# The last output tile of a linear-attention block: one add moved to GpSimd, two adds and two stores joined

## The chip, the cores and the metric

The kernel runs on one core of a Trainium2 chip. The metric is the device time of one execution in microseconds (us), the median over several runs. A core has five engines that run their own instruction streams and wait for each other through semaphores: TensorE (PE, matmuls and weight loads), VectorE (DVE), ScalarE (ACT), GpSimd (POOL) and SyncE (SP). SP only issues DMAs here; ACT issues some too.

## The reference

The input x has 2048 tokens of 640 features. It is normalised, goes through a linear attention with 32 heads and through a two-layer network with a ReLU, and the two results are combined with a residual:

```
xn = layernorm(x)
q, k, v = split(xn @ wqkv)                  # 32 heads of 20
phi(t) = where(t > 0, t + 1, exp(t)) + 1e-6
o = phi(q) @ (phi(k)^T @ v) / (phi(q) . sum(phi(k)) + 1e-6)
s = o @ wo
g = silu(relu(xn @ w1) @ w2)                # 1728 hidden features
out = x + s * g
```

## The kernel before

The kernel is written instruction by instruction. A small scheduler class (`Sched`) takes every operation in program order, with the resources that it reads (`R`) and writes (`W`), and works out which semaphores the issuing engine has to wait for. Each engine executes its own operations in the order in which they were written. A wait blocks everything behind it on the same engine. The same holds for a DMA: the engine whose queue issues it (SP or ACT) first waits for the data. Every DMA has a semaphore of its own, and at the very end SP waits for all of them (`wait_all_dma`).

The tokens form 16 tiles of 128 rows. The last stage works through pairs of tiles. For each tile, `U_sub` and `U_halves` (matmuls at L846 and L864) compute the network's second layer into PSUM, `gate` (L874, ScalarE) writes `g` = silu of it to SBUF as bf16, and then the output is made. A matmul group `s_mm` (L895) computes s for the tile: five matmuls per column piece, with the folded weight `wf`, into one PSUM bank. `s_out` then does three things for a piece of columns: VectorE multiplies the PSUM result by g into `tmpo` (L885), VectorE adds the residual x (`xre`) into `outb` (L888), and SP stores `outb` to the output in HBM (L891).

Where these output parts stand among the matmuls of the second layer is a table written out by hand (`hooks`). Fifteen tiles are done by `s_tile`, with two matmul groups of 320 columns, one multiply, one add and one store of all 640 columns. The sixteenth is done last, by `s_last`, and cut into three pieces of 224, 208 and 208 columns, each with its own PSUM bank, multiply, add and store:

```
LC = [0, 224, 432, 640]
LB = [2, 3, 4]
```

For the last tile all matmuls of the second layer are over before `s_mm` begins, and its g is written by the last `gate`. `NOUT` is the slot of `tmpo` and `outb` that only the last tile uses. Other lines that the text names are: L414 and L416 (statistics of the layer norm on VectorE and GpSimd), L501 (GpSimd's running sum of phi(k)), L525 (VectorE's sum that makes phi(k)) and L551 (a VectorE operation whose input tensor is in PSUM).

Of the kernel before, what the change touches and what calls it, by code (L numbers as in the profile page):

```python
# [4 lines left out]
ALU = mybir.AluOpType  # L5
# [15 lines left out]
class Sched:  # L21
# [69 lines left out]

    def _hazards(self, R, W):
        agents = []
        for key in R:
            st = self.res.get(key)
            if st is not None and st.w is not None:
                agents.append(st.w)
        for key in W:
            st = self.res.get(key)
            if st is not None:  # L100
                if st.w is not None:
                    agents.append(st.w)
                agents.extend(st.r.values())
        return agents

    def _update_res(self, agent, R, W):
        Rset = set(R)
        for key in R:
            st = self.res.get(key)
            if st is None:  # L110
                st = self.res[key] = _Res()
            rk = agent if agent[0] == "D" else agent[0]
            st.r[rk] = agent
            st.nread += 1
        for key in W:
            st = self.res.get(key)
            if st is None:
                st = self.res[key] = _Res()
            else:
                assert (st.w is None or st.nread > 0 or key in Rset or key in self.allow_unread  # L120
                        or (agent[0] == "PE" and st.w[0] == "PE")), (
                    "unread overwrite of %r by %r (prev writer %r)" % (key, agent, st.w))
            st.w = agent
            st.r = {}
            st.nread = 0

    def op(self, E, fn, R=(), W=(), extra=()):
        return self.group(E, [fn], R, W, extra)
# [80 lines left out]
def bass_recurrent_scan__linear_attn_block__dense_activation_relu__prompt_kernel(  # L209
# [9 lines left out]
    Bb, S, D = A_x.shape  # L219
# [11 lines left out]
    HN = D // 2  # L231
# [6 lines left out]
    out2 = out[0]  # L238
# [10 lines left out]
    xre = xn  # L249

    NOUT = 4
# [4 lines left out]
    outb = reg3[:, VC * D:(VC + NB) * D].rearrange("p (a n) -> p a n", a=NB)  # L256
    tmpo = reg3[:, (VC + NB) * D:(VC + 2 * NB) * D].rearrange("p (a n) -> p a n", a=NB)
# [50 lines left out]
    ps = [psT[:, 512 * i:512 * (i + 1)] for i in range(8)]  # L308

    def ps2(b, n):  # L310
        return psT[:, 512 * b:512 * (b + 2)].rearrange("p (a n) -> p a n", a=2)[:, :, 0:n]
# [4 lines left out]
    sc = Sched(nc, NDS)  # L316
    nds = [0]

    def dma(E, fn, R=(), W=(), extra=()):
        i = nds[0]  # L320
        nds[0] += 1
        return sc.dma(E, fn, i, R=R, W=W, extra=extra)

    def tok(t):
        return slice(P * t, P * (t + 1))
# [25 lines left out]
    def wk_load(k0, k1):  # L351
# [23 lines left out]
          R=[("ident",)], W=[("ident",)])  # L375
# [344 lines left out]
    for j in range(J):  # L720
        for n, item in enumerate(plans[j]):
# [21 lines left out]
            if n in kat[j]:  # L743
                t = kat[j][n]
# [10 lines left out]
            if j == J - 1 and n == 0:  # L755
                for c in range(VC):
                    r0 = VR * c if c < VC - 1 else D - P
                    dma("SP", lambda eng, c=c, r0=r0: eng.dma_start(wo_sb[:, c, :], A_wo[r0:r0 + P, :]),
                        W=[("wo", c)], extra=[last_norm[0]])
# [12 lines left out]
    for a in range(2):  # L772
# [3 lines left out]
            W=[("w2", a)], extra=[lastW1])  # L776
    for u in range(2):
        dma("ACT", lambda eng, u=u: eng.dma_start(w2l[64 * u:64 * (u + 1), :], B_w2[NF * P:FF, :]),
            W=[("w2l", u)], extra=[lastW1])
# [100 lines left out]
    LC = [0, 224, 432, 640]  # L880
    LB = [2, 3, 4]

    def s_out(t, os_, i, lo, hi, src, keys, na):
        shp = "p (a n) -> p a n"
        sc.op("DVE", lambda eng: eng.tensor_tensor(  # L885
            out=tmpo[:, os_, lo:hi].rearrange(shp, a=na), in0=src, in1=g_sb[:, t, lo:hi].rearrange(shp, a=na),
            op=ALU.mult), R=keys + [("g", t)], W=[("tmpo", os_, i)])
        sc.op("DVE", lambda eng: eng.tensor_tensor(out=outb[:, os_, lo:hi], in0=tmpo[:, os_, lo:hi],  # L888
                                                   in1=xre[:, t, lo:hi], op=ALU.add),
              R=[("tmpo", os_, i), ("xre", t // 4)], W=[("outb", os_, i)])  # L890
        dma("SP", lambda eng: eng.dma_start(out2[tok(t), lo:hi], outb[:, os_, lo:hi]), R=[("outb", os_, i)])  # L891

    def s_mm(t, lo, hi, b):
        i = t // 4
        sc.group("PE", [(lambda eng, c=c: eng.matmul(  # L895
            ps[b][:, 0:hi - lo], lhsT=pqT[:, c, tok(t)], rhs=wf[:, c, lo:hi],
            start=(c == 0), stop=(c == C - 1))) for c in range(C)],
            R=[("pqT", i, c) for c in range(C)] + wkeys, W=[("ps", b)])

    def s_tile(t, b):  # L900
        os_ = so[0] % NOUT
        so[0] += 1
        for a in range(2):
            s_mm(t, HN * a, HN * (a + 1), b + a)
        s_out(t, os_, 0, 0, D, ps2(b, HN), [("ps", b), ("ps", b + 1)], 2)

    def s_last(t):
        for i in range(3):
            lo, hi = LC[i], LC[i + 1]
            s_mm(t, lo, hi, LB[i])  # L910
            s_out(t, NOUT, i, lo, hi, ps[LB[i]][:, 0:hi - lo].unsqueeze(1), [("ps", LB[i])], 1)

    lastG = None
    for k in range(C):
# [1 line left out]
    for jx in range(4):  # L916
        dma("SP", lambda eng, jx=jx: eng.dma_start(
            xre[:, 4 * jx:4 * jx + 4, :], x2[512 * jx:512 * (jx + 1), :].rearrange("(t p) n -> p t n", p=P)),
            W=[("xre", jx)], extra=[lastG])

    def s_of(p, u, b):
        return lambda: s_tile(pairs[p][u], b)
# [29 lines left out]
    for p in range(8):  # L952
# [7 lines left out]
        if p % 2 == 0:  # L960
            U_halves(p)
            gate(p, 0)
            gate(p, 1)
    s_last(pairs[7][1])

    sc.wait_all_dma("SP", list(range(nds[0])))
# [30 lines left out]
```

## Time and profile before

| | us |
|---|---|
| median of 5 runs | 221.24 |
| lowest and highest | 221.06, 221.47 |
| the profiled execution's own time | 221.23 |
| its span, from the first to the last instruction | 220.0 |
| TensorE busy | 214.8 (98%) |
| VectorE busy | 119.8 (54%) |
| ScalarE busy | 83.6 (38%) |
| GpSimd busy | 43.4 (20%) |

The granted TensorE clock was 0.998 over the span. In the rows of the profile a line is written as L885, an engine by its short name, and a queue that issues DMAs with a q behind it (SPq, ACTq). Operands are written output<-input with the names of the tensors: `reg` stands for the large SBUF regions, in which `tmpo`, `outb`, `g` and `xre` lie, and `psT` for PSUM. A group's row gives the shapes as partitions x elements, a count, then the busy time in us and the mean length of one in ns, and then the idle time in front. A row of the timeline gives the start in us, the length in us, and what ran.

### The profile page before, as it was taken

The page shows a single profiled execution, that of the slowest core. Times are in us where ns is not written, and L with a number is a line of the kernel's source. Part 1 is how long each engine was busy: PE and PEld are TensorE (multiplying, and loading weights), DVE is VectorE, ACT ScalarE, POOL GpSimd, SP SyncE. Part 2 cuts the span into 40 slices and gives each one's busy share as a digit, 9 for nine tenths or more (in the row PEclk, how much of TensorE's full clock was granted, in tenths as well). Part 3 has the DMA queues.
Part 4 walks back from the last instruction along what each step waited for, and adds up shares of the span by engine and source line. Part 5 has one row for each costly group of instructions (what it writes and reads, how often), then busy time and mean ns, then how long its engine had stood idle before and what let it go on. Part 6 is the DMA issues. An engine that isn't in the chain of part 4 may idle for free.

```text
span 220.0 us, 3506 instructions
## 1 busy us (share of the span) xinstructions
PE 214.8 (98%) x1436; PEld 132.9 (60%) x1436; DVE 119.8 (54%) x222; ACT 83.6 (38%) x139; POOL 43.4 (20%) x68
## 2 busy tenths in 40 slices
PE   6999999999999999999999999999999999999994
PEld 6555554555545555444467777677767776777673
DVE  3999947789639999783702116930424240413234
ACT  4497665566665676554420000551021102110211
POOL 2278501120041699950000000000000000000000
PEclk9999999999999999999999999999999999999999
DMA  6987493811001243000099979922110100001011
GB/s 215 365 236 160 96 317 37 208 30 30 3 1 35 54 105 107 0 0 3 5 207 308 370 234 376 368 77 63 50 40 30 63 30 30 33 30 61 3 60 60
DMA packets 28565, 24.72 MB, mean 112 GB/s; under 512 B 12293, under 2 KB 27909, under 8 KB 28549
## 3 DMA queue, kind: packets, MB, share of 16 engines
q1 hardware_dynamic: 24965, 19.83, 31.6%
q10 hardware_dynamic: 3584, 4.67, 6.3%
q8 instruction: 11, 0.18, 0.3%
q14 instruction: 5, 0.04, 0.1%
HBM read 15.81 MB, written 5.24 MB: 96 GB/s over the span
## 4 chain that ended last, share of the span: by engine, by line
PE 95%; DVE 2%; DMA 1%; ACT 0%; issue 0%; DVEq 0%
PE psT L846 26%; PE psT L565 26%; PE psT L786 10%; PE psT L543 10%; PE psT L490 10%; PE psT L895 9%; DMA reg<-in_A_x_dram 1%; PE psT L864 1%; PE psT L582 1%; PE psT L816 1%; PE psT L801 1%; PE psT L673 1%; DVE regX L475 0%; PE psT L465 0%; DVE reg L885 0%; DVE stats L410 0%
## 5 line engine op out<-in xcount | busy, mean ns | idle before, releaser
L846 PE MATMUL psT<-reg,hT 128*128 128x320 bf16 x416 | 60.5, 299 | 0.0
L846 PEld LDWEIGHTS psT<-reg,hT 128*128 128x128 bf16 x416 | 40.3, 98 | 16.4 <-issue 1.1
L565 PE MATMUL psT<-reg 128*128 128x512 bf16 x195 | 46.0, 379 | 0.0
L885 DVE TENSOR_TENSOR reg<-psT,reg 128x640 bf16<-128x640 f32 (+2 forms) x18 | 13.5, 750 | 48.3 <-PE psT L895 47.0
L569 ACT ACTIVATE hT<-psT 128x512 bf16<-128x512 f32 x52 | 30.8, 604 | 18.2 <-PE psT L565 18.2
L565 PEld LDWEIGHTS psT<-reg 128*128 128x128 bf16 x195 | 18.9, 98 | 21.8 <-issue 0.4
L874 ACT ACTIVATE reg<-psT 128x640 bf16<-128x640 f32 x12 | 8.2, 702 | 44.7 <-PE psT L846 25.3
L543 PE MATMUL psT<-reg 128*128 128x512 bf16 x100 | 24.8, 379 | 0.0
L895 PE MATMUL psT<-reg,pqT 128*128 128x320 bf16 (+2 forms) x165 | 24.4, 295 | 0.0
L501 POOL TENSOR_TENSOR zacc<-zacc,reg 128x640 f32<-128x640 f32 x16 | 23.8, 1488 | 2.3 <-DVE reg L525 1.3
L786 PE MATMUL psT<-reg 128*128 128x320 bf16 x160 | 21.9, 299 | 0.0
L895 PEld LDWEIGHTS psT<-reg,pqT 128*128 128x128 bf16 x165 | 16.1, 98 | 5.8
L786 PEld LDWEIGHTS psT<-reg 128*128 128x128 bf16 x160 | 15.7, 98 | 6.2
L507 ACT ACTIVATE regE<-psT 128x640 bf16<-128x640 f32 x24 | 15.6, 701 | 9.1 <-PE psT L490 7.6
L490 PE MATMUL psT<-reg 128*128 128x320 bf16 x120 | 18.3, 299 | 0.0
L551 DVE TENSOR_SCALAR regE<-psT 128x512 bf16<-128x512 f32 x20 | 13.6, 679 | 8.2 <-ACT regE L550 8.2
L553 DVE SCALAR_TENSOR_TENSOR pqT<-regE 128x512 bf16<-128x512 bf16 x20 | 17.4, 869 | 0.7
L543 PEld LDWEIGHTS psT<-reg 128*128 128x128 bf16 x100 | 9.8, 98 | 11.6
L410 DVE BATCH_NORM_STATS2 stats<-reg 128x6 f32<-128x320 bf16 x32 | 14.2, 476 | 2.8 <-DMA reg<-in_A_x_dram 2.8
L490 PEld LDWEIGHTS psT<-reg 128*128 128x128 bf16 x120 | 11.7, 98 | 6.5 <-DMA reg<-reg 0.2
L791 DVE CAST reg<-psT 128x640 bf16<-128x640 f32 x5 | 4.1, 825 | 20.9 <-PE psT L786 20.9
L550 ACT ACTIVATE regE<-psT 128x512 bf16<-128x512 f32 x20 | 11.9, 597 | 8.8 <-PE psT L543 8.8
(67 smaller groups left out, 162.1 us busy)
## 6 DMA issues: line engine op xcount, KB each, us to landing
scr<-regE SPq DMA_DIRECT2D x4, 640.0 KB, 11.1
reg<-in_A_x_dram SPq DMA_DIRECT2D x4, 640.0 KB, 9.3
out_dram<-reg SPq DMA_DIRECT2D x15, 160.0 KB, 1.8
reg<-in_A_x_dram SPq DMA_DIRECT2D x13, 160.0 KB, 4.0
regE<-scr SPq DMA_DIRECT2D x4, 512.0 KB, 5.6
reg<-in_B_w_dram ACTq DMA_DIRECT2D x1, 1120.0 KB, 12.1
reg<-in_B_w_dram ACTq DMA_DIRECT2D x1, 1040.0 KB, 6.3
reg<-in_A_wo_dram SPq DMA_DIRECT2D x6, 160.0 KB, 3.2
```

The lines of the kernel that those rows point to most:

```text
L410: sc.op("DVE", lambda eng: eng.bn_stats(stats[:, t, a, :], xv[:, HN * a:HN * (a + 1)]), R=[("xin", t % XR)], W=[("stats", t, a)])
L490: fns.append(lambda eng, a=a, k=k, lhs=lhs: eng.matmul(ps[b + a][:, 0:HN], lhsT=lhs[:, k, tok(t)], rhs=wqk[:, k, D + HN * a:D + HN * (a + 1)],
L501: sc.op("POOL", lambda eng: eng.tensor_tensor(out=zacc[:, :], in0=zacc[:, :], in1=pk[:, t, :], op=ALU.add), R=[("zacc",), ("pk", t)], W=[( ...
L507: sc.op("ACT", lambda eng: eng.activation(out=o_.rearrange("p (a n) -> p a n", a=2), in_=ps2(b, HN), func=func, scale=scale), R=[("ps", b) ...
L543: sc.group("PE", [(lambda eng, k=k: eng.matmul(ps[b], lhsT=wqk[:, k, P * f:P * (f + 1)], rhs=xnT[:, k, schunk(j)], start=(k == 0), stop=(k ...
L551: sc.op("DVE", lambda eng: eng.tensor_scalar(out=r_, in0=ps[b], scalar1=0.0, scalar2=1e-6, op0=ALU.max, op1=ALU.add), R=[("ps", b), ("er_e ...
L553: sc.op("DVE", lambda eng: eng.scalar_tensor_tensor(out=pqT[:, f, schunk(j)], in0=e_, scalar=1.0, in1=r_, op0=ALU.min, op1=ALU.add), R=[(" ...
L565: a = sc.group("PE", [(lambda eng, k=k: eng.matmul(ps[b], lhsT=w1_sb[:, k, P * f:P * (f + 1)], rhs=src[:, k, :], start=(k == 0), stop=(k = ...
L569: sc.op("ACT", lambda eng: eng.activation(out=hT[:, f, schunk(j)], in_=ps[b], func=ACTF.Relu), R=[("ps", b)], W=[("hT", j, f)])
L786: fns.append(lambda eng, t=t, a=a: eng.matmul(ps[b + a][:, 0:HN], lhsT=xn[:, t, P * k:P * (k + 1)], rhs=pk[:, t, HN * a:HN * (a + 1)], sta ...
L846: sc.group("PE", [(lambda eng, f=f: eng.matmul(ps[b][:, 0:HN], lhsT=hT[:, f, tok(t)], rhs=w2_sb[:, f, HN * n:HN * (n + 1)], start=(f == 0 ...
L895: sc.group("PE", [(lambda eng, c=c: eng.matmul(ps[b][:, 0:hi - lo], lhsT=pqT[:, c, tok(t)], rhs=wf[:, c, lo:hi], start=(c == 0), stop=(c = ...
```

## The change

The multiply of a piece (`s_mult`) and the add with the store (`s_store`) become two functions. `s_store` takes the pieces that it waits for, the range of columns, the engine of the add and the queue of the store. The fifteen earlier tiles issue what they did before. In the last tile the add of the first piece (224 columns) goes to GpSimd and its store to ScalarE's queue; the second and third pieces get a common add on VectorE (416 columns) and a common store from SP, behind the third multiply.

```diff
-    def s_out(t, os_, i, lo, hi, src, keys, na):
+    def s_mult(t, os_, i, lo, hi, src, keys, na):
         shp = "p (a n) -> p a n"
         sc.op("DVE", lambda eng: eng.tensor_tensor(
             out=tmpo[:, os_, lo:hi].rearrange(shp, a=na), in0=src, in1=g_sb[:, t, lo:hi].rearrange(shp, a=na),
             op=ALU.mult), R=keys + [("g", t)], W=[("tmpo", os_, i)])
-        sc.op("DVE", lambda eng: eng.tensor_tensor(out=outb[:, os_, lo:hi], in0=tmpo[:, os_, lo:hi],
-                                                   in1=xre[:, t, lo:hi], op=ALU.add),
-              R=[("tmpo", os_, i), ("xre", t // 4)], W=[("outb", os_, i)])
-        dma("SP", lambda eng: eng.dma_start(out2[tok(t), lo:hi], outb[:, os_, lo:hi]), R=[("outb", os_, i)])
+
+    def s_store(t, os_, pieces, lo, hi, E="DVE", D_="SP"):
+        sc.op(E, lambda eng: eng.tensor_tensor(out=outb[:, os_, lo:hi], in0=tmpo[:, os_, lo:hi],
+                                               in1=xre[:, t, lo:hi], op=ALU.add),
+              R=[("tmpo", os_, i) for i in pieces] + [("xre", t // 4)], W=[("outb", os_, lo)])
+        dma(D_, lambda eng: eng.dma_start(out2[tok(t), lo:hi], outb[:, os_, lo:hi]), R=[("outb", os_, lo)])
...
-        s_out(t, os_, 0, 0, D, ps2(b, HN), [("ps", b), ("ps", b + 1)], 2)
+        s_mult(t, os_, 0, 0, D, ps2(b, HN), [("ps", b), ("ps", b + 1)], 2)
+        s_store(t, os_, (0, ), 0, D)
 
     def s_last(t):
         for i in range(3):
             lo, hi = LC[i], LC[i + 1]
             s_mm(t, lo, hi, LB[i])
-            s_out(t, NOUT, i, lo, hi, ps[LB[i]][:, 0:hi - lo].unsqueeze(1), [("ps", LB[i])], 1)
+            s_mult(t, NOUT, i, lo, hi, ps[LB[i]][:, 0:hi - lo].unsqueeze(1), [("ps", LB[i])], 1)
+            if i == 0:
+                s_store(t, NOUT, (0, ), lo, hi, "POOL", "ACT")
+        s_store(t, NOUT, (1, 2), LC[1], D)
```

## The prediction

> **What bounds the kernel now.** I read the page's chain first, then the chain in order of time over the last microseconds, then the groups by form for prices, the DMA view for the stores, and last the timeline of an earlier stage where VectorE (DVE) and GpSimd (POOL) worked at once. The page's rows say that TensorE carries the kernel and that GpSimd has nothing to do in the last half:
>
> ```profile
> PE   6999999999999999999999999999999999999994
> ...
> POOL 2278501120041699950000000000000000000000
> ...
> PE 95%; DVE 2%; DMA 1%; ACT 0%; issue 0%; DVEq 0%
> ```
>
> The change touches only what follows the last matmuls, so only the tail counts. The chain in order of time (start us, length us, what):
>
> ```profile
> 213.89 1.78 PE psT L846 x13
> ...
> 215.69 0.71 ACT reg L874
> ...
> 216.50 0.40 DVE reg L885
> 216.90 0.02 issue
> 216.93 0.28 DVE reg L888
> 217.20 0.29 DVE reg L885
> 217.50 0.02 issue
> 217.52 0.27 DVE reg L888
> 217.78 0.30 DVE reg L885
> 218.08 0.02 issue
> 218.10 0.27 DVE reg L888
> ```
>
> The reader is to see that from the end of the last gate (L874) on, VectorE alone holds the end, with three pairs of multiply (L885) and add (L888). TensorE is finished earlier: its last 15 matmuls (L895) start at 215.49 and take 1.53, so they end at 217.02. After the last add (218.10 + 0.27 = 218.37) the SP queue issues the last store at 218.40; 1.5 us later it has landed, and the span ends at 220.0. In the DMA view:
>
> ```profile
> out_dram<-reg SPq DMA_DIRECT2D x15, 160.0 KB, 1.8
> ...
> out_dram<-reg SPq DMA_DIRECT2D x2, 52.0 KB, 1.6
> out_dram<-reg SPq DMA_DIRECT2D x1, 56.0 KB, 1.5
> ```
>
> The last number is us from issue to landing. Seen alone, the two 52 KB stores take 1.6 and, the last one, 1.5.
>
> **VectorE, on the path.** The change removes two of the three adds, adds one of 416 columns, and lets the three multiplies follow each other. Prices, from the groups by form of the last 5 us:
>
> ```profile
> L885 DVE TENSOR_TENSOR reg<-psT,reg 128x208 bf16<-128x208 f32 x2 | 0.7, 368 | 0.0
> ...
> L888 DVE TENSOR_TENSOR reg<-reg 128x208 bf16<-128x208 bf16 x2 | 0.5, 266 | 0.1
> L888 DVE TENSOR_TENSOR reg<-reg 128x640 bf16<-128x640 bf16 x1 | 0.5, 493 | 0.0
> ```
>
> The first multiply stays at 216.50 to 216.89 (the gate sets it). The second waits for nothing on VectorE. In the timeline of before the second multiply starts at 217.12 while the add in front of it runs from 216.93 to 217.21: an independent instruction starts 0.09 before its predecessor's end. So the second runs 216.80 to 217.17 and the third 217.08 to 217.45; its matmuls end at 217.02, a margin of 0.06. The joint add depends on the third multiply and starts 0.03 later, as adds do in the chain: 217.48. Its length lies between the rows of 208 and 640 columns: (493 - 266) / 432 = 0.525 ns a column, 266 + 208 x 0.525 = 375 ns. It ends at 217.86 instead of 218.37, which is 0.51 earlier.
>
> **The last store.** SP issues one store at 217.89 in place of three; the issue (0.33) and the wait at the end stay, two issues and two landings that were hidden go. The new store has 104 KB against 52. By the rows, 1.55 at 52 KB and 1.8 at 160 KB, it takes 1.55 + 0.25 x 52/108 = 1.67, that is +0.12. Against this row stands a rule of the Trainium skill: "DMA: Bandwidth & Descriptors", Specifications, says that under 512 bytes a transfer is not at line rate, because the engine reads, modifies and writes. The old pieces have rows of 416 and 448 bytes, the new one 832, so by the rule the growth would be nothing. No row here has the new size. By the row the gain is 0.39, by the rule 0.51; I take +0.05, gain 0.46, and keep both ends.
>
> **GpSimd's add and ScalarE's store, meant to lie beside this.** The tile's first add now waits on GpSimd for the first multiply (216.89). Earlier GpSimd followed VectorE by 0.09 (L414 ends at 10.41, L416 starts at 10.50), so it starts at 216.98. Its length has no row at 224 columns. The nearest is L501, 640 columns at 1.40 undisturbed. In proportion that is 0.49; with a fixed part as large as the whole one-column L416 (0.22) it is 0.22 + 224 x 1.18/640 = 0.63. I take 0.56; it ends at 217.54, between 217.47 and 217.61. ScalarE finished its last gate at 216.39; nothing is queued behind its wait, nor behind GpSimd's. Its store is issued at 217.57, 217.66 at the latest. The two loads of 160 KB issued together at 0.79 landed after 3.0 (SP) and 3.2 (ScalarE), so I give it 1.5 to 1.7: it lands by 219.1 to 219.4. The main store lands at 217.89 + 1.55 + 0.05 = 219.49. The first store is hidden with 0.1 to 0.4 to spare; past that its delay counts in full. The two issues overlap by at most 0.1 (about 0.35 each, 217.57 and 217.89); those at 0.79 took 0.40 and about 0.45 instead of 0.33 to 0.37, so that price is 0 to 0.1; I take 0, as the second hardly touches the first.
>
> **The port.** GpSimd's add and VectorE's joint add may meet at 217.48. The timeline shows what that does:
>
> ```profile
> 22.13 0.49 DVE L525 TENSOR_TENSOR reg<-regE 128x640 bf16<-128x640 bf16 x1
> ...
> 22.76 1.40 POOL L501 TENSOR_TENSOR zacc<-zacc,reg 128x640 f32<-128x640 f32 x1 [0.85 <-DVE reg L525]
> 22.89 1.62 DVE L525 TENSOR_TENSOR reg<-regE 128x640 bf16<-128x640 bf16 x1
> ```
>
> The same VectorE add takes 0.49 alone and 1.62 when it starts inside GpSimd's: it ends 0.35 after GpSimd does (24.16 to 24.51). So it is held to the end of GpSimd's add, and then needs 0.14 less than its usual length. For the joint add this gives GpSimd's end + 0.23 = 217.70 to 217.84, not later than its own 217.86: no cost, as long as GpSimd's add lasts under 216.98 + d + 0.23 < 217.86, d < 0.65. The Trainium skill, "SBUF — State Buffer", "A bandwidth-pool intuition that's wrong", speaks against the change more strongly: work of GpSimd that VectorE locks out is blocked until VectorE ends plus about 115 ns, and only then runs. Taken for the opposite order too, that would be 217.54 + 0.115 + 0.375 = 218.03, and the gain 0.46 - 0.17 = 0.29. The row is of this pair of operations, so I take it and keep the rule's 0.17 in the range.
>
> Whether the multiplies too are held, or hold GpSimd, no row shows: L551, whose only tensor is in PSUM, keeps its 0.69 inside L501 (at 92.68), but the multiply reads PSUM and SBUF. Bound below: nothing. Above: GpSimd waits for the third multiply, 217.45 + 0.56 = 218.01, and the joint add ends at 218.24. I take nothing, since one SBUF operand leaves the pair of the row above incomplete.
>
> **Sum.** -0.51 + 0.05 = -0.46 on the profiled execution's 221.23 (span 220.0, 1.23 around it): 220.77. Its time is 0.01 under the median of the runs, which changes nothing.
>
> **The rivals.**
> 1. The multiplies share the port with GpSimd. For: they read SBUF. Against: L551 is untouched. The joint add ends at 218.24, the gain is 0.13 - 0.05 = 0.08: 221.15, no change.
> 2. GpSimd's add is long and holds VectorE's last add, the one on the path. GpSimd has slept since 96.6, some 120 us; the longest idle before one of its operations in the trace is 13.1, and its first L416 took 0.40 against 0.22. From d = 0.65 on every ns goes to the end; at 0.65 + 0.46 = 1.11 the gain is used up. With the 1.40 that 640 columns took the result is 221.23 + 0.29 = 221.52; with 1.73, the longest L501, 221.85. Against: the add has a third of those columns, and the spans of GpSimd are rough in both directions.
> 3. The change doesn't do what it says: ScalarE's store lands last. It needs a landing over 1.9 us from 217.57; the only store sizes seen take 1.5 to 1.8, the loads of the start that took 3.2 shared the engines with megabytes. If it took 3.2, the end is 220.8 and the time 222.05. I count it with rival 2.
>
> **How the numbers follow.** A difference under 0.2% (0.44 us) is about what a measurement of this kernel can tell from no change. My case has 0.74; its own range is 220.55 to 220.98 (gain 0.29 to 0.51, and some 0.1 between runs), and its centre lies just past the bound, the store's size decides: 0.50 beyond and 0.24 within. Rival 1 has 0.08, within. Rivals 2 and 3 have 0.18, of which 0.02 stays within. Faster 0.50, same 0.34, slower 0.16. The range reaches from 220.55 to 221.55, which takes in rival 1 and rival 2 at 1.40; longer adds and a late ScalarE store are left out.
>
> **What would show it.** Right: three L885 rows closing up from 216.5 to 217.45; one add of 416 columns of about 0.38 starting at 217.48; a GpSimd add of 0.49 to 0.63; ScalarE's store landed first; the span near 219.5. Wrong: a joint add of over 0.4 that ends 0.23 after GpSimd's (the port); multiplies longer than 0.39 or GpSimd starting after 217.4 (rival 1); a last wait of SP for ScalarE's store; a landing of over 1.7 for the 104 KB store.

## The result and the profile after

The changed kernel takes 220.87 us in the median of 43 runs (220.59 to 222.25), the kernel before 221.29 in 80 runs beside it (221.02 to 223.28). The difference of the medians is 0.42 us or 0.19%; the ratio is 0.9975 with a 95% interval of [0.9965, 0.9985]. The interval lies below one, so the changed kernel is faster. Whether it is so by more than the 0.2% that the prediction set as its bound is open: the interval reaches from 0.15% to 0.35%, and the medians lie just short of the bound. The lowest times of the two differ by 0.43.

The profiled execution of the changed kernel took 222.22, its span is 221.0, a whole us longer than the span before. Of either kernel some executions are about 1.4 us longer (16 of the 80 before and 5 of the 43 after are over 222), and this profile caught one of them; the last section shows where in the trace that time lies. So the two tails are not compared by the clock of the span, but from a common mark, the start of the last gate (L874), which is at 215.69 before and at 217.08 after. In what follows "the tail" is the time from that mark to the end of the span. It was 4.29 us before and is 3.91 after, 0.38 shorter. In the changed kernel the lines behind L885 have moved: the add is L890, the store L893 and the matmuls of `s_mm` L897.

The page's rows, as shown of before: TensorE and its share of the chain are as they were, GpSimd has one mark in the last slice.

```profile
PE   7999999999999999999999999999999999999995
...
POOL 2177701111032499970000000000000000000001
...
PE 96%; DMA 1%; DVE 1%; ACT 0%; issue 0%; DVEq 0%
```

The chain in order of time (start us, length us, what):

```profile
215.27 1.78 PE psT L846 x13
...
217.08 0.71 ACT reg L874
...
217.88 0.96 DVE reg L885 x3
218.85 0.02 issue
218.87 0.37 DVE reg L890
```

The three multiplies are one block of 0.96 and one add follows. VectorE's part ends at 219.24, 2.17 behind the mark, where it ended 2.68 behind it before: 0.51 less. GpSimd is nowhere in the chain. The timeline of the last stretch shows it beside VectorE:

```profile
218.19 0.65 DVE L885 TENSOR_TENSOR reg<-psT,reg 128x208 bf16<-128x208 f32 x2
218.35 0.61 POOL L890 TENSOR_TENSOR reg<-reg 128x224 bf16<-128x224 bf16 x1 [120.41 <-DVE reg L885]
...
218.87 0.37 DVE L890 TENSOR_TENSOR reg<-reg 128x416 bf16<-128x416 bf16 x1
218.99 0.36 ACTq L893 DMA_DIRECT2D out_dram<-reg  x1
219.27 0.33 SPq L893 DMA_DIRECT2D out_dram<-reg  x1
```

GpSimd woke 0.08 after the first multiply's end (218.27), after 120.41 us of idleness, and ran to 218.96. ScalarE issued its store at 218.99, SP its own at 219.27. In the DMA view (the last number is us from issue to landing) the joint store is what grew:

```profile
out_dram<-reg SPq DMA_DIRECT2D x1, 104.0 KB, 1.7
out_dram<-reg ACTq DMA_DIRECT2D x1, 56.0 KB, 1.6
```

In the trace's events the joint store lands 1.66 after its issue, the last store of before 1.54 after its own. The books of the tail close: -0.51 on VectorE, +0.12 on the store, -0.38 measured, with 0.01 of rounding.

The prices by form in the last us answer to those of before. Two multiplies that overlap GpSimd have the length they had, 365 against 368 ns:

```profile
L885 DVE TENSOR_TENSOR reg<-psT,reg 128x208 bf16<-128x208 f32 x2 | 0.6, 365 | 0.0
...
L890 POOL TENSOR_TENSOR reg<-reg 128x224 bf16<-128x224 bf16 x1 | 0.6, 607 | 120.4 <-DVE reg L885 120.4
...
L890 DVE TENSOR_TENSOR reg<-reg 128x416 bf16<-128x416 bf16 x1 | 0.4, 374 | 0.0
```

### The profile page after: what moved, and what is told of

Same layout as the page of the kernel before. It is cut to its first block, busy times and chain, and to the rows that moved or that the text cites. A ratio compares the mean times of both kernels' runs of the same rounds, so it can differ in the third digit from the quotient of the medians.

```text
span 221.0 us, 3503 instructions
## 1 busy us (share of the span) xinstructions
PE 216.6 (98%) x1436; PEld 134.1 (61%) x1436; DVE 119.5 (54%) x220; ACT 83.6 (38%) x139; POOL 43.8 (20%) x69
## 4 chain that ended last, share of the span: by engine, by line
PE 96%; DMA 1%; DVE 1%; ACT 0%; issue 0%; DVEq 0%
PE psT L846 26%; PE psT L565 25%; PE psT L490 11%; PE psT L786 10%; PE psT L543 10%; PE psT L897 9%; DMA reg<-in_A_x_dram 1%; PE psT L864 1%; PE psT L582 1%; PE psT L465 1%; PE psT L816 1%; PE psT L801 1%; PE psT L673 1%; DVE reg L885 0%; ACT reg L874 0%; DVE stats L410 0%
## 5 line engine op out<-in xcount | busy, mean ns | idle before, releaser
L885 DVE TENSOR_TENSOR reg<-psT,reg 128x640 bf16<-128x640 f32 (+2 forms) x18 | 13.3, 750 | 48.3 <-PE psT L897 47.0
L874 ACT ACTIVATE reg<-psT 128x640 bf16<-128x640 f32 x12 | 8.2, 702 | 44.7 <-PE psT L846 25.3
L890 POOL TENSOR_TENSOR reg<-reg 128x224 bf16<-128x224 bf16 x1 | 0.6, 607 | 120.4 <-DVE reg L885 120.4
L897 PE MATMUL psT<-reg,pqT 128*128 128x320 bf16 (+2 forms) x165 | 24.4, 295 | 0.0
L501 POOL TENSOR_TENSOR zacc<-zacc,reg 128x640 f32<-128x640 f32 x16 | 23.8, 1488 | 2.3 <-DVE reg L525 1.3
L897 PEld LDWEIGHTS psT<-reg,pqT 128*128 128x128 bf16 x165 | 16.1, 98 | 5.8
L490 PE MATMUL psT<-reg 128*128 128x320 bf16 x120 | 18.3, 299 | 0.0
L490 PEld LDWEIGHTS psT<-reg 128*128 128x128 bf16 x120 | 11.7, 98 | 6.5 <-DMA reg<-reg 0.2
```

Source lines behind the costliest of these rows:

```text
L490: fns.append(lambda eng, a=a, k=k, lhs=lhs: eng.matmul(ps[b + a][:, 0:HN], lhsT=lhs[:, k, tok(t)], rhs=wqk[:, k, D + HN * a:D + HN * (a + 1)],
L501: sc.op("POOL", lambda eng: eng.tensor_tensor(out=zacc[:, :], in0=zacc[:, :], in1=pk[:, t, :], op=ALU.add), R=[("zacc",), ("pk", t)], W=[( ...
L897: sc.group("PE", [(lambda eng, c=c: eng.matmul(ps[b][:, 0:hi - lo], lhsT=pqT[:, c, tok(t)], rhs=wf[:, c, lo:hi], start=(c == 0), stop=(c = ...
```

## The experiments

All variants differ from the changed kernel in the last tile alone. Because the effects are a tenth to half a us, the intervals of the ratios hold the value one in most of them, and the times do not tell the variants apart. The readings rest on the tail in the traces. It repeats within 0.01 us for the changed kernel, which was traced twice (3.91 and 3.91); the others were traced once each. What all traces have in common agrees as closely: the first multiply starts 0.81 behind the mark in each of them but gate_halves, and the 160 KB store in front of the tail lands 1.78 to 1.79 after its issue in all.

| kernel | tail, us | less than before | ratio to before, 95% interval |
|---|---|---|---|
| before | 4.29 | | |
| the change | 3.91 | 0.38 | 0.9975 [0.9965, 0.9985] |
| join_only | 4.20 | 0.09 | 0.9992 [0.9966, 1.0018] |
| pool_only | 4.20 | 0.09 | 0.9991 [0.9962, 1.0020] |
| one_add | 4.14 | 0.15 | 0.9992 [0.9959, 1.0025] |
| pool_sp | 4.08 | 0.21 | 0.9997 [0.9966, 1.0028] |
| two_adds | 4.09 | 0.20 | 1.0000 [0.9967, 1.0033] |
| two_adds_sp | 4.21 | 0.08 | 0.9984 [0.9955, 1.0013] |
| gate_halves | 3.78 | 0.51 | 0.9976 [0.9951, 1.0000] |
| change_again | 3.91 | 0.38 | 0.9973 [0.9948, 0.9998] |

**join_only: the joining without GpSimd.**

```diff
-                s_store(t, NOUT, (0, ), lo, hi, "POOL", "ACT")
+                s_store(t, NOUT, (0, ), lo, hi)
```

> The joint add and store of pieces 2 and 3, but the first piece's add back on VectorE, directly behind its multiply, and its store back on SP. Tail from the start of the last gate (L874) to the end of the span: 4.29 us before, 3.91 after the change. My theory: the first add stands between the first two multiplies again (0.23 us of VectorE's chain; chain 216.50, 216.93, 217.12, 217.40, joint add 217.80 to 218.18), the store keeps its 1.66, so the tail is 4.22, a gain of 0.07 of the 0.38. Rival (the gain is the joining: one add and one store fewer behind each other, GpSimd adds nothing): tail 3.9 to 4.0.

Measured: tail 4.20. The chain in order of time shows the first add back between the multiplies:

```profile
216.91 0.40 DVE reg L885
217.31 0.02 issue
217.34 0.28 DVE reg L890
217.61 0.58 DVE reg L885 x2
218.19 0.02 issue
218.21 0.38 DVE reg L890
```

VectorE's part ends 2.48 behind the mark, 0.31 later than with the change, and the larger store eats most of what is left of the gain. Joining alone is worth 0.09 us; the rival that it is the whole gain falls.

**pool_only: GpSimd without the joining.**

```diff
             if i == 0:
                 s_store(t, NOUT, (0, ), lo, hi, "POOL", "ACT")
-        s_store(t, NOUT, (1, 2), LC[1], D)
+            else:
+                s_store(t, NOUT, (i, ), lo, hi)
```

> The first piece's add on GpSimd and its store from ScalarE, as in the change; pieces 2 and 3 with an add and a store each, as before. My theory (GpSimd's add holds a VectorE add with two SBUF operands): the second piece's add comes at 217.20 (clock of the profile before), in the middle of GpSimd's 0.61, and is held to GpSimd's end + 0.12: its row shows 0.5 instead of 0.27; the third multiply and add follow, tail 4.21, gain 0.08. Rival (no hold at these sizes): the add's row stays at 0.27 and the tail is 3.97. Rival (the gain is GpSimd's and ScalarE's part alone): tail 3.9.

Measured: tail 4.20. The timeline shows the hold that the prediction had feared for the joint add: a VectorE add that starts while GpSimd's runs does not end until GpSimd's has. It falls on the second piece's add, which comes while GpSimd is at work:

```profile
216.73 0.61 POOL L890 TENSOR_TENSOR reg<-reg 128x224 bf16<-128x224 bf16 x1 [120.41 <-DVE reg L885]
216.96 0.49 DVE L890 TENSOR_TENSOR reg<-reg 128x208 bf16<-128x208 bf16 x1
...
217.77 0.27 DVE L890 TENSOR_TENSOR reg<-reg 128x208 bf16<-128x208 bf16 x1
```

Two adds of one shape: 0.49 inside GpSimd's add, 0.27 after it. The held one ends 0.12 after GpSimd, as worked out from the rows of L525 and L501 (usual length less 0.14). So the two halves of the change need each other. By these rows GpSimd's add is free only if no VectorE operation with two SBUF operands is due more than about 0.14 before its end (the joint add of the change is due 0.09 before it), and the joining puts two multiplies, which are not held, into exactly that gap. Singly they give 0.09 each, together 0.38.

**one_add: all three adds in one, no GpSimd.**

```diff
-            if i == 0:
-                s_store(t, NOUT, (0, ), lo, hi, "POOL", "ACT")
-        s_store(t, NOUT, (1, 2), LC[1], D)
+        s_store(t, NOUT, (0, 1, 2), 0, D)
```

> No GpSimd and no ScalarE store: three multiplies on VectorE, then one add of 640 columns and one SP store of 160 KB. My theory: the multiplies close up as in the change, the add is 0.49 instead of 0.37, the store lands 1.78 after its issue instead of 1.66: tail 3.91 + 0.12 + 0.12 = 4.14. That is the price of leaving GpSimd out in the best order for VectorE. Rival (what counts is the number of instructions and stores at the end): 3.9 or less.

Measured: tail 4.14, as expected. Its chain is the change's with a longer last add:

```profile
217.07 0.96 DVE reg L885 x3
218.03 0.02 issue
218.06 0.49 DVE reg L890
```

and its store of 160 KB lands 1.78 after the issue instead of 1.66. Against this kernel GpSimd and ScalarE are thus worth 0.23: 0.12 in the add and 0.12 in the store, which they make smaller, less 0.01 of rounding. Another order without GpSimd was not run: the joint add and its store first, then the first piece's add on VectorE with its store from ScalarE. As an estimate from these traces, that add (0.28) would end at about 2.36 behind the mark, and its store (issued 0.03 later, landing after 1.59) would end the tail at about 4.0. So what GpSimd itself brings may be nearer to 0.1.

**pool_sp: the first store from SP.**

```diff
-                s_store(t, NOUT, (0, ), lo, hi, "POOL", "ACT")
+                s_store(t, NOUT, (0, ), lo, hi, "POOL", "SP")
```

> As the change, but the first piece's store is issued by SP instead of ScalarE. My theory: SP issues it at GpSimd's end + 0.03 for 0.33 us, so the joint store's issue moves by 0.05 to 0.08: tail 3.97. Rival (two queues share the descriptor work, one after the other costs nothing or is better, as the ScalarE issue took 0.365 against 0.333): 3.91 or less. Rival (two stores in one queue stand behind each other): 4.1 or more.

Measured: tail 4.08, more than my 3.97. VectorE is unchanged (joint add to 2.17 behind the mark). SP issues the first store at 220.20 for 0.33, and the joint store 0.04 after that issue has ended:

```profile
220.57 0.43 SPq L893 DMA_DIRECT2D out_dram<-reg  x1
```

This issue takes 0.43, and in the DMA view, which counts from the issue's start, the joint store lands later than the 1.66 of the change:

```profile
out_dram<-reg SPq DMA_DIRECT2D x1, 104.0 KB, 1.8
```

(1.75 in the events.) The issue is 0.09 later and the landing 0.09 longer, together the 0.18 by which this tail is longer. The longer landing is the longer issue itself: from the end of the issue the store takes 1.32, with the change 1.33. ScalarE's queue, which I had costed at some 0.06, is worth 0.18. The next two runs ask whether it is the issue right behind another one.

**two_adds and two_adds_sp: the joint add and store taken apart.**

```diff
-        s_store(t, NOUT, (1, 2), LC[1], D)
+        s_store(t, NOUT, (2, ), LC[2], D)
+        s_store(t, NOUT, (1, ), LC[1], LC[2], "DVE", "ACT")
```

and in two_adds_sp the last line without `"DVE", "ACT"`.

> As the change, but behind the three multiplies the joint add and store are taken apart: the third piece's add with its store from SP, then the second piece's add with its store from ScalarE's queue, behind the first piece's. Times from the start of the last gate; tail 3.91 with the change. Third piece's add 1.80 to 2.06, store issued by SP at 2.09; second piece's add 1.98 to 2.25. Theory A (an issue that follows another at once in the same queue is stretched and lands later, as with pool_sp, where the second issue took 0.43 instead of 0.33 and landed after 1.75 instead of 1.66): ScalarE's second store is issued at about 2.32 for 0.43 and lands after 1.63, tail 4.0. Theory B (the 0.18 of pool_sp came from the size or from chance): the small store lands after 1.54, tail 3.87, better than the change.

> As two_adds, but both of its stores come from SP, one behind the other (issues at 2.09 and about 2.44 from the last gate's start). Theory A: the second issue takes 0.43 and lands after 1.63, tail 4.11. Theory B: 0.33 and 1.54, tail 4.03.

Measured: tails 4.09 and 4.21, each 0.1 longer than even theory A had it. The second issue of one queue, ScalarE's in two_adds and SP's in two_adds_sp, starts 0.04 after the end of the one in front of it, and takes 0.44 and 0.43:

```profile
218.09 0.44 ACTq L893 DMA_DIRECT2D out_dram<-reg  x1
```

```profile
218.09 0.43 SPq L893 DMA_DIRECT2D out_dram<-reg  x1
```

The first issue on the same queue took 0.36 and 0.33. So the stretch is seen on both queues and for three sizes of pairs. Where a gap of 0.25 lies between the issues, as before the change, the row is 0.33 each time. The landing is the part that theory A undersized: 52 KB took 1.73 and 1.70 instead of 1.54, where 1.63 was expected. Of the 0.19 and 0.16, the longer issue is 0.11 and 0.10; the other 0.08 and 0.06 come after the issue's end. Stores that move at the same time show such a delay without any close issue in their own queue: SP's first store, with an issue of the usual 0.33, lands after 1.63 and 1.62 here, and in pool_only, where ScalarE's store had been issued 0.12 before it, 52 KB took 1.75 in the events. No run isolates this share.

```profile
217.48 0.33 SPq L893 DMA_DIRECT2D out_dram<-reg  x1
...
out_dram<-reg SPq DMA_DIRECT2D x1, 52.0 KB, 1.8
```

What follows for the change: one joint store, costing 0.12 more in its landing, was the better choice, since two smaller ones cost more, at the issue and in the landing.

**gate_halves: a version from the same reading.** With the change VectorE's chain starts when the last gate of 0.71 is over, though the first piece needs only its columns, and one of the two PSUM banks is complete earlier.

```diff
+    def gate_half(p, u, n):
+        t = pairs[p][u]
+        b = ubase(p) + 2 * u + n
+        sc.op("ACT", lambda eng: eng.activation(out=g_sb[:, t, HN * n:HN * (n + 1)], in_=ps[b][:, 0:HN],
+                                                func=ACTF.Silu, scale=1.0), R=[("ps", b)], W=[("g", t, n)])
...
-    LC = [0, 224, 432, 640]
+    LC = [0, 256, 480, 640]
...
+        gk = [("g", t)] if os_ < NOUT else [("g", t, 0)] if hi <= HN else [("g", t, 0), ("g", t, 1)]
...
-            op=ALU.mult), R=keys + [("g", t)], W=[("tmpo", os_, i)])
+            op=ALU.mult), R=keys + gk, W=[("tmpo", os_, i)])
...
-                if p % 2 == 1 and n == 1:
+                if p == 7 and u == 1:
+                    gate_half(p, u, n)
+                elif p % 2 == 1 and n == 1:
                     gate(p, u)
```

> The change with two edits: the last tile's gate is cut into its two PSUM banks (320 columns each), so that the first half runs during the second half's matmuls, and the pieces are 256, 224 and 160 columns. It stays one add on GpSimd and one joint add (384 columns). Theory: the first multiply no longer waits for 0.71 of gate but for the first piece's matmuls; the chain is then set by the last matmuls (end 1.34 from the start of the last gate half): multiplies 0.57, 1.03 and 1.37 to 1.69, joint add 1.72 to 2.08, store of 96 KB 1.64: tail 3.79 against 3.91. Rival (the end stays bound by VectorE's chain alone, or ScalarE's half gate takes longer than 0.46 and holds the second multiply): 3.9 or more.

Measured: tail 3.78. The chain in order of time no longer has ScalarE in it; it runs from the matmuls of the pieces (in this kernel L904) to the multiplies (L892) and the joint add (L897):

```profile
216.70 1.04 PE psT L904 x10
217.74 0.02 issue
217.76 0.68 DVE reg L892 x2
218.44 0.02 issue
218.47 0.36 DVE reg L897
```

That is 0.12 to 0.13 less than the two traces of the change. In the times it can't be told from the change: medians 221.08 and 220.97 on the same chip, ratios 0.9976 and 0.9973 with intervals of 0.5%. One trace shows the gain, the times do not confirm it.

**change_again: the changed kernel beside the last three.**

> The changed kernel itself beside the three others on the same chip: tail 3.91, ratio 0.998 against the kernel before.

Measured: tail 3.91, ratio 0.9973 [0.9948, 0.9998], as in the first comparison.

## Why the prediction was right, and where a step was off

The predicted 220.77 is 0.10 under the measured median, and the forecast gain of 0.46 stands against 0.42 in the medians and 0.38 in the tail. Of the 0.10, 0.06 is that the median before is 221.29 in this comparison, and not the 221.23 from which the prediction counted; that the medians come so near to 0.46 is partly luck, as the tail is the better measure. The mechanism came as forecast; one term of the sum had the wrong size.

- **VectorE's chain** was right in every row. Counted from the first multiply's start, the third was to end at 0.95 and ended at 0.96; the joint add was to take 375 ns and took 374; the end was to come 0.51 earlier and did. An add's length at a new width can be interpolated between two rows of the same form.
- **The last store** is the mis-sized term. The row gave +0.12, my reading of the Trainium skill's rule on transfers under 512 bytes ("DMA: Bandwidth & Descriptors", Specifications) gave nothing, and I took +0.05 between them. The row was right to the hundredth: 1.54 at 52 KB, 1.66 at 104, 1.78 at 160 KB. No advantage of the rows of 832 bytes over those of 416 shows in these landings; the rule speaks of the rate of a transfer, and that the growth would be nothing was my own step from it. Had the row alone been used, the gain would have been 0.39.
- **GpSimd's add** was to take 0.49 to 0.63, 0.56 in the middle; it took 0.607. The upper bound, with a fixed part as in L416, was the nearer one: with 1.40 at 640 columns (L501, float32 there) and 0.67 at 256 in gate_halves the three rows lie on 0.18 us plus 1.90 ns a column. It started 0.08 behind its multiply after 120 us of idleness, so rival 2 fell, though narrowly: the add stayed 0.04 under the 0.65 from which every ns would have gone to the end.
- **The port** cost nothing, and the row decided against the sharper reading of the Trainium skill ("SBUF — State Buffer", "A bandwidth-pool intuition that's wrong"). That page's sentence is about a DMA whose descriptors GpSimd has to write, and carrying it over to an add of VectorE was the prediction's own step. GpSimd ended at 218.96, 0.09 after the joint add had started; held to GpSimd's end + 0.23 it would end at 219.19, and its own 219.24 is later, by 0.05. The 115 ns and a full length behind them would have given 219.45. Whether the joint add was held at all can't be seen here; pool_only shows the same bookkeeping where the hold does bite.
- **Rival 1**, multiplies that share the port, fell: the second and third multiply keep their length under GpSimd's add, and GpSimd starts in the middle of one. The prediction had taken nothing for them without a row that showed it; the runs bear it out.
- **Rival 3**, ScalarE's store landing last, fell: 1.59 from issue to landing, inside the 1.5 to 1.7, and 0.36 before the joint one. The prediction saw in it only a hidden path, though. Its real worth is to SP's queue, which is free when the joint store comes: 0.18 by pool_sp.
- **Slips that change nothing:** ScalarE's issue at 0.79 took 0.41, not about 0.45 (the second one, at 1.24, took 0.46); the latest issue of its store is 217.64 by the prediction's own numbers, not 217.66; and gains of 0.29 to 0.51 with 0.1 to either side give 220.62 to 221.04, not 220.55 to 220.98.

## What to carry to other kernels

At the end of a kernel, read the chain engine by engine: an add moved to an idle engine gains only what the order of the rest lets it gain, and here neither the moved add (0.09) nor the joined one (0.09) was worth much without the other (0.38 together). Give GpSimd an operation for a stretch in which each of VectorE's operations has at most one SBUF input, as the multiplies here, and check its end against the next VectorE operation with two SBUF inputs. Size a last store by rows of the same queue, and keep it from standing directly behind another issue there.

## What the runs showed of the hardware that was not expected

An issue that starts 0.04 us after the last one of its queue takes 0.43 to 0.44 us instead of 0.33 to 0.37, on SP and on ScalarE alike, and its store, counted from the start of the issue, lands 0.09 to 0.19 later than one of its size behind a free queue. About 0.1 of that is the longer issue itself; the rest is seen only where a third store moves. Issues of one queue with a gap of 0.25 don't show it. Nor does the other queue bring it about by itself: with the change, SP's issue starts 0.08 before ScalarE's has ended and takes 0.33. In pool_only, where the two overlap by 0.28, ScalarE's takes 0.40.

The 1.4 us by which the trace after is longer at the mark lie at its start, where both kernels issue the same work. Ten matmuls of one line (L490, 320 columns) are in the timelines, before and then after:

```profile
6.27 1.79 PE L490 MATMUL psT<-reg,regX 128*128 128x320 bf16 x10
```

```profile
6.78 2.87 PE L490 MATMUL psT<-reg,regX 128*128 128x320 bf16 x10
```

The same matmuls take 2.87 us instead of 1.79 (474 ns for one instead of 299), although the granted clock is given as 1.00 in both traces there. Both traces begin with the longer lengths. Before, a matmul of 128 columns goes from 311 to 220 ns at 4.1 us; after, it goes from 314 to 219 at 9.7 us. From 10.3 us on the distance between the two traces stays at 1.38 us. No run here shows what sets that moment. The 1.4 us are three times the effect of this change, which is why the tail, and not the span, had to be read.
